# Attention, ELU projection and maxout layer on one core: order of stores, turns, splits and copies changed in the last three stages

## The chip, the cores and the metric

The kernel runs on one core of a Trainium2 chip. A core has TensorE (matmuls out of SBUF into PSUM), VectorE, ScalarE, GpSimd and SyncE, each with its own queue of instructions that it works off in order, and DMA engines that move data between HBM and SBUF. The metric is device time of one execution in microseconds (us). Before the change it is 539.83 us, the median of three runs (538.1 to 540.93).

## The reference

Three stages, all in float32 (the weight arrays of the second and third come as 64-bit floats):

```python
# 1. causal attention, batch 2, 12 heads, sequence 448, head size 64
scores = where(mask, -1e9, scale * q @ k.T)
attn = exp(scores - max(scores)); attn = attn / (sum(attn) + 1e-9)
x = (attn @ v) laid out as [896 tokens, 768]
# 2. ELU layer: 768 -> 2048 -> 768
h = x @ w_in                       # [896, 2048]
x = where(h > 0, h, exp(min(h, 0)) - 1) @ w_out
# 3. maxout layer: 768 -> 768 -> 768
h = maximum(maximum(x @ w1, x @ w2), x @ w3)
out = h @ w_out2                   # [896, 768]
```

## The kernel before, in words

**Products in three parts.** Each float32 operand is split into a high half (what TensorE's reduced format keeps, written by ScalarE) and a low half (the rest, a subtraction on VectorE); `split` (L129) does both. A product is then three matmuls: high x high, high x low, low x high.

**64-bit weights.** `load64` (L76) fetches a panel of 64-bit floats into a tile of the ring "raw" (three slots, L78). `conv64` (L87) turns it into float32 words: two ScalarE instructions (L91, L92) and two on VectorE in `join` (L96, L97). `conv_split` (L108) is `conv64` and `split` one behind the other. `weight_tile` is a ring of three ("ws"), `word_tile` a ring of two ("c").

**Stages.** Attention runs by a plan that is written out by hand. The ELU stage (L599 to L614) goes over 16 panels of w_in; 36 matmuls of a panel (`h_unit`, L350) give 128 columns of the hidden layer, which stay in SBUF. This stage is ordered by the framework's own scheduler. Everything behind L643 stands in a block of manual order: each engine gets its instructions in the order of the program.

**First output projection ("py", L667 to L693).** 24 panels of w_out (512 KB in HBM each): `load_wout(n + 3)`, `split_wout(n + 2)`, then 24 matmuls (L684) on panel n. Every four panels a block of 128 output columns is complete in PSUM; `y_copy` (ScalarE, L641) brings the block before to SBUF, and `y_first` or `y_sums` derive operands from it.

**Blocks turned in advance.** The 18 blocks of w1, w2 and w3 (768 KB each) are loaded beside the ELU and the py stage (`load_later`), turned into float32 (`turn_later`, two instructions on each of ScalarE and VectorE, into the one "ce" tile) and stored to a scratch area in HBM (L127). The store is issued by SyncE, in the same queue as the panel loads.

**Maxout stage.** The 896 tokens and the blocks are cut in 2 x 2 and multiplied with seven products in place of eight (x1 to x7, `product`, L746, nine matmuls each, L755). There are nine units n: `load_quad` (L708) fetches four quarter blocks of a unit from scratch, `split_first` splits two of them, `weight_sums` forms four sums and differences, `split_sums` and `split_last` split those. x1, x6, x7 and x4 add up in one PSUM bank, from which ScalarE copies the state after each (`keep_p`, `keep_u`, `keep_v`): the next product must not start before the copy. `result` and `result_x` add and take maxima on VectorE. `turn_half` (L854) loads, between the units, a half panel of w_out2 and turns it.

**Between py and the units** (L811 to L841) the operands that depend on the last y block are made; the last `y_copy` stands behind the splits there.

**Final stage.** `quadrant` and `rest` (L983) multiply by w_out2, again with seven products; `fill` splits an operand into a slot, the answers are added on VectorE and stored.

## Time and profile before

| | us |
|---|---|
| median of three runs | 539.83 |
| profiled execution | 542.84 |
| its span, first to last instruction | 541.0 |
| TensorE matmul busy | 491.7 (91%) |
| TensorE weight loads busy | 419.5 (78%) |
| VectorE busy | 386.8 (71%) |
| ScalarE busy | 316.7 (59%) |
| mean granted TensorE clock | 0.968 |

The profile is of one execution. In its rows PE is TensorE, PEld its weight loads, DVE VectorE, ACT ScalarE, POOL GpSimd, SP (SPq) the queue of SyncE; L350 is line 350 of the kernel. A row in order of time gives the start and the length in us, engine, line and operation, output<-input by the names in the program, and how many instructions it merges; in brackets stands the idle time of that engine before it and what ended it. A row of a window gives its start and end, its length, then busy time and count of PE, PEld, DVE, ACT and POOL, the granted TensorE clock (1.00 is 2.4 GHz), the DMA share and GB/s. Matmuls overlap, so the mean of one is longer than the distance from one to the next.

### The profile page before, as it was taken

What the parts mean: (1) busy time and instruction counts of PE and PEld (TensorE: products, weight loads), DVE (VectorE), ACT (ScalarE), POOL (GpSimd) and SP (SyncE); (2) the same over time, 40 slices, a digit from 0 to 9 for tenths busy, and PEclk for the clock granted to TensorE, in tenths of its full rate; (3) what the DMA queues carried; (4) which work ended last, traced back from release to release, by engine and by line L of the source; (5) the groups of instructions that cost most, each with busy time, mean ns of one, the idle gap of its engine ahead of it and who ended that gap; (6) DMA issues with size and microseconds to landing.
All of it is one profiled execution on the core that took longest, in us unless ns stands there. A gap on an engine that the chain in (4) does not pass through costs nothing.

```text
span 541.0 us, 7502 instructions
## 1 busy us (share of the span) xinstructions
PE 491.7 (91%) x2677; PEld 419.5 (78%) x2677; DVE 386.8 (71%) x759; ACT 316.7 (59%) x649; POOL 50.2 (9%) x104
## 2 busy tenths in 40 slices
PE   9999999999999999999988899029998999988997
PEld 5777677799999988898776677019987888878896
DVE  4999897698778786565555555286677777798874
ACT  4999897698888876354463553344434444334430
POOL 1656447000000000000000000000000000000000
PEclk9999999999999999999999999658999999998989
DMA  9996210158655450566665554522333332000104
GB/s 199 249 219 149 62 34 2 59 175 259 207 187 177 152 176 29 168 195 209 195 199 190 167 166 136 179 103 87 110 113 90 91 114 97 2 1 1 44 16 145
DMA packets 81509, 69.69 MB, mean 129 GB/s; under 512 B 35136, under 2 KB 75328, under 8 KB 81472
## 3 DMA queue, kind: packets, MB, share of 16 engines
q1 hardware_dynamic: 80544, 68.99, 43.3%
q8 instruction: 21, 0.34, 0.3%
q10 hardware_dynamic: 928, 0.23, 0.2%
q14 instruction: 16, 0.13, 0.1%
HBM read 59.38 MB, written 9.83 MB: 128 GB/s over the span
## 4 chain that ended last, share of the span: by engine, by line
PE 45%; DVE 21%; DMA 13%; ACT 13%; issue 4%; POOL 2%; SPq 1%; ACTq 0%; DVEq 0%; POOLq 0%
PE ph L350 21%; DMA raw_o<-in_moe_w_out_dram 7%; PE py L684 5%; PE s L227 4%; PE te L290 4%; DMA wx<-in_moe_w_out_dram 3%; DVE c_t L638 3%; PE av L315 3%; PE bx L755 3%; ACT wb L130 3%; POOL e L280 2%; DVE ce L96 2%; DVE ce L97 2%; ACT raw_e L92 2%; DMA out_dram<-o 1%
## 5 line engine op out<-in xcount | busy, mean ns | idle before, releaser
L684 PE MATMUL py<-gs,ws_o 128*128 128x512 f32 (+1 forms) x576 | 123.4, 369 | 8.0 <-ACT ws_o L130 6.4
L684 PEld LDWEIGHTS py<-gs,ws_o 128*128 128x128 f32 x576 | 102.8, 188 | 28.5 <-ACT ws_o L130 12.0
L350 PE MATMUL ph<-x,ws_l 128*128 128x512 f32 (+2 forms) x576 | 118.7, 365 | 0.0
L350 PEld LDWEIGHTS ph<-x,ws_l 128*128 128x128 f32 x576 | 103.9, 188 | 12.5 <-issue 1.0
L280 POOL TENSOR_SCALAR e<-e,r 112x336 f32<-112x336 f32 (+3 forms) x96 | 48.9, 528 | 42.6 <-DVE r L274 41.9
L261 ACT ACTIVATE e<-e,nm 112x448 f32<-112x448 f32 (+3 forms) x96 | 49.7, 526 | 3.3 <-DVE nm L247 3.1
L755 PE MATMUL bx<-ops_a_s,ws_a 128*128 128x448 f32 x81 | 20.7, 409 | 23.3 <-ACT y L641 23.3
L247 DVE CUSTOM_DVE_ANT_0 e<-s,mask 112x224 f32<-112x224 f32 (+3 forms) x96 | 37.8, 441 | 3.1 <-PE s L227 3.0
L755 PE MATMUL by<-ops_s,wb 128*128 128x448 f32 x162 | 36.9, 374 | 1.8 <-DVE r L638 1.8
L130 ACT ACTIVATE ws_o<-c_o 128x512 fp32r<-128x512 f32 x24 | 15.1, 630 | 39.8 <-DVE c_o L97 36.7
L755 PEld LDWEIGHTS bx<-ops_a_s,ws_a 128*128 128x128 f32 x81 | 17.5, 217 | 25.4 <-ACT y L641 23.7
L96 DVE SCALAR_TENSOR_TENSOR c_o<-c_o,raw_o 128x512 uint32<-128x512 uint32 x24 | 16.5, 688 | 25.4 <-ACT raw_o L92 25.4
L755 PEld LDWEIGHTS by<-ops_s,wb 128*128 128x128 f32 x162 | 30.9, 191 | 4.8 <-DVE r L638 2.2
L130 ACT ACTIVATE wb<-c_t 128x768 fp32r<-128x768 f32 x18 | 14.2, 836 | 26.9 <-DVE c_t L638 26.9
L96 DVE SCALAR_TENSOR_TENSOR ce<-ce,raw_e 128x768 uint32<-128x768 uint32 x18 | 17.2, 957 | 17.2 <-ACT raw_e L92 17.1
L131 DVE TENSOR_TENSOR ws_o<-c_o,ws_o 128x512 fp32r<-128x512 f32 x24 | 16.6, 692 | 18.0 <-ACT ws_o L130 18.0
L290 PE MATMUL te<-ident,e 112*112 112x112 f32 x240 | 27.7, 261 | 1.4 <-POOL e L280 1.2
L91 ACT ACTIVATE c_o<-raw_o 128x512 f32<-128x512 f32 x24 | 15.9, 664 | 20.2 <-DMA raw_o<-in_moe_w_out_dram 18.8
L290 PEld LDWEIGHTS te<-ident,e 112*112 112x112 f32 x240 | 23.8, 133 | 4.3 <-POOL e L280 2.8
L755 PE MATMUL bx<-ops_a,wb 128*128 128x448 f32 x81 | 18.8, 376 | 7.6 <-ACT v L641 7.6
L227 PE MATMUL s<-qk 64*112 64x224 f32 (+3 forms) x192 | 24.9, 405 | 0.0
L315 PE MATMUL av<-et,vn 112*64 112x448 f32 (+3 forms) x192 | 24.4, 403 | 0.0
(167 smaller groups left out, 862.1 us busy)
## 6 DMA issues: line engine op xcount, KB each, us to landing
raw_e<-in_moe_w_dram SPq DMA_DIRECT2D x18, 768.0 KB, 6.2
raw_l<-in_moe_w_in_dram SPq DMA_DIRECT2D x16, 768.0 KB, 4.7
raw_o<-in_moe_w_out_dram SPq DMA_DIRECT2D x24, 512.0 KB, 4.8
turned<-ce SPq DMA_DIRECT2D x18, 384.0 KB, 2.8
quad<-turned SPq DMA_DIRECT2D x18, 384.0 KB, 4.2
wx<-in_moe_w_out_dram SPq DMA_DIRECT2D x12, 384.0 KB, 3.1
qn<-in_q_dram SPq DMA_DIRECT2D x24, 112.0 KB, 3.8
vn<-in_v_dram SPq DMA_DIRECT2D x12, 224.0 KB, 3.9
```

The source lines that it names most:

```text
L96: nc.vector.scalar_tensor_tensor(r, r, 3, low, ALU.logical_shift_left, ALU.bitwise_or)
L130: nc.scalar.activation(hi, src, AF.Copy)
L131: nc.vector.tensor_tensor(lo, src, f32(hi), ALU.subtract)
L227: nc.tensor.matmul(s[j][:C, o : o + (c + 1) * C], qk[:, a, c * C : (c + 1) * C], qk[:, c2, : (c + 1) * C], start=(w == 0 and n == 0), stop ...
L247: nc.vector.tensor_tensor_reduce(out=e_t[h][:, EOFF[c] : EOFF[c] + (c + 1) * C], in0=ps_now.pop(("s", h, c)), in1=mask[:, (NCH - 1 - c) * ...
L261: nc.scalar.activation(e, e, AF.Exp, bias=nm_t[h][:, c : c + 1], scale=-1.0, accum_out=sm_t[p][:, j, c : c + 1],)
L280: nc.gpsimd.tensor_scalar(e, e, ps_now["r", h][:, c : c + 1], 1.0, ALU.mult, ALU.mult)
L290: nc.tensor.transpose(t[:C, n : n + C], e[:, EOFF[c] + j * C : EOFF[c] + (j + 1) * C], ident[:C, :C],)
L315: nc.tensor.matmul(a[j * D : (j + 1) * D, kc * C : S], vn[:, j * NCH + kc, :], et[j][:, TOFF[kc] : TOFF[kc] + S - kc * C], start=(n == 0), ...
L350: nc.tensor.matmul(ps, w(a, kc), x(c, kc), start=(i == 0), stop=(i == len(seq) - 1))
L684: nc.tensor.matmul(py[m, b][:, : at.stop - at.start], w[:, a, kc * P : (kc + 1) * P], g_sp[hk * HK + kc][:, c, at], start=(hk == 0 and i = ...
L755: nc.tensor.matmul(bank[:, :S], w, side[:, c, k, :], start=(not onto and k == 0 and (a, c) == (0, 0)), stop=(k == K2 - 1 and (a, c) == (1, ...
```

## The change

- Of the three "raw" slots two stay in the ring and one ("apart") is kept for the blocks turned in advance, for w_in panel 2, for every third quad and for the tile v of the final stage.
- Blocks are loaded at every odd panel of the ELU stage. In the py stage a block's store, and behind it the next block's load, are issued at the start of the panel after the turn; blocks are turned at odd panels.
- `conv_split` of a w_out panel is parted: in panel n the kernel splits panel n + 2, turns panel n + 3 and loads panel n + 5.
- The first three quads are loaded in the last panels of the py stage; between py and the units `split_first(0)`, `weight_sums(0)` and `split_first(1)` come first.
- In a unit, `turn_half`, `keep_v` and the c11 result go ahead of the sums' splits; the second `turn_half` goes ahead of x2.
- The last two units are written out and interleaved. The final stage's operand preparation is moved about, and the copy of l1 goes ahead of the t4 subtraction.

```diff
@@ -73,9 +73,12 @@
     NW = KD * P
     BIAS = 2.0**-112
 
-    def load64(key, src, n):
-
-        t = cv.tile([P, NW, 2], U32, tag="raw", bufs=3, name=f"raw_{key}")
+    def raw_tile(name, apart=False):
+        tag, bufs = ("apart", 1) if apart else ("raw", 2)
+        return cv.tile([P, NW, 2], U32, tag=tag, bufs=bufs, name=name)
+
+    def load64(key, src, n, apart=False):
+        t = raw_tile(f"raw_{key}", apart)
         k_n = src.shape[0] // P
         nc.sync.dma_start(
             t[:, :n, :].rearrange("p (k e) w -> p k (e w)", k=k_n),
@@ -112,17 +115,21 @@
     K2 = KF2 // 2
     scratch = ctx.enter_context(tc.tile_pool(name="scratch", bufs=1, space=DRAM))
     later = [(j + n * K2, i) for j in range(K2) for i in range(3) for n in range(2)]
-    loaded, turned = [], {}
+    loaded, leaving, turned = [], [], {}
 
     def load_later():
         m, i = later.pop(0)
-        raw = load64(f"e{m}_{i}", (w1, w2, w3)[i][:, m * P : (m + 1) * P], NW)
+        raw = load64(f"e{m}_{i}", (w1, w2, w3)[i][:, m * P : (m + 1) * P], NW, True)
         loaded.append((m, i, raw))
 
     def turn_later():
         m, i, raw = loaded.pop(0)
         c = cv.tile([P, NW], U32, tag="ce", bufs=1, name=f"ce{m}_{i}")
         conv64(raw, c, NW)
+        leaving.append((m, i, c))
+
+    def store_later():
+        m, i, c = leaving.pop(0)
         turned[m, i] = scratch.tile([P, NW], F32, name=f"turned{m}_{i}")
         nc.sync.dma_start(turned[m, i], f32(c[:, :]))
...
@@ -605,7 +612,8 @@
                 split_win(i, f"l{i}", f < 2)
         if loaded:
             turn_later()
-        if f > 3 and f % 2 == 0:
+            store_later()
+        if f % 2 == 1:
             load_later()
...
+    def turn_wout(i):
+        pan[i] = conv64(pan[i], word_tile(f"o{i}"), HK * P)
+
     def split_wout(i):
-        pan[i] = conv_split(f"o{i}", pan[i], HK * P)
-
-    for i in range(3):
-        load_wout(i)
-    for i in range(2):
-        split_wout(i)
+        c, pan[i] = pan[i], weight_tile(f"o{i}")
+        split(pan[i][:, 0, : HK * P], pan[i][:, 1, : HK * P], c)
+
+    load_wout(0)
+    load_wout(1)
+    turn_wout(0)
+    load_wout(2)
+    split_wout(0)
+    turn_wout(1)
+    load_wout(3)
+    split_wout(1)
+    turn_wout(2)
+    load_wout(4)
...
+        def load_quad(n):
+            j, i = ITEMS[n]
+            t = raw_tile(f"quad{n}", n % 3 == 2)
+            quads[n] = t = f32(t.rearrange("p n w -> p (n w)")).rearrange(
+                "p (q e) -> p q e", q=4
+            )
+            for x in range(2):
+                nc.sync.dma_start(
+                    t[:, 2 * x : 2 * x + 2].rearrange("p q e -> p (q e)"), turned[j + x * K2, i]
+                )
+
         for n in range(NP):
             m, hk = divmod(n, NQ)
-            if n + 3 < NP:
-                load_wout(n + 3)
+            if leaving:
+                store_later()
+                if later:
+                    load_later()
             if n + 2 < NP:
                 split_wout(n + 2)
-            if loaded:
+            if n + 3 < NP:
+                turn_wout(n + 3)
+            if n + 5 < NP:
+                load_wout(n + 5)
+            if n >= NP - 4 and n < NP - 1:
+                load_quad(n - NP + 4)
+            if n % 2 == 1 and loaded:
                 turn_later()
-            if hk % 2 == 0 and later:
-                load_later()
             if hk == 0:
...
+        split_first(0)
+        weight_sums(0)
+        split_first(1)
         part("a01", slice(0, 2), y[:, 3:5, T[0]])
         part("s2", slice(0, 2), y[:, 0:2, T[0]])
-        load_quad(0)
-        load_quad(1)
-        weight_sums(0)
-        split_first(0)
-        load_quad(2)
         part("s1", slice(0, 2), y[:, 0:2, T[1]])
         part("a11", slice(0, 2), y[:, 3:5, T[1]])
+        split_sums(0)
+        split_last(0)
         add(y[:, 3:5, T[0]], y[:, 3:5, T[0]], y[:, 0:2, T[0]], ALU.subtract)
         part("s4", slice(0, 2), y[:, 3:5, T[0]])
-        split_first(1)
-        split_sums(0)
-        split_last(0)
         y_copy(KD - 1)
...
-        for n in range(NI):
+        for n in range(NI - 2):
+            x6(n)
             if n > 0:
-                result(n - 1, 0, 1, U.pop(n - 1), Y.pop(n - 1))
+                result_c01(n - 1)
             if n + 3 < NI:
                 load_quad(n + 3)
-            if n + 2 < NI:
-                split_first(n + 2)
-            if n == NI - 2:
-                first_tiles()
-                for k in range(K2):
-                    first_part(k, 0)
-
-            Y[n] = bank3("by", n)
-            product("x5", n, Y[n], False)
+            split_first(n + 2)
+            x5(n)
             keep_u(n)
-            if n + 1 < NI:
-                weight_sums(n + 1)
-            if n == NI - 1:
-                tx = late.tile([P, 3, K2, DMO], F32, tag="wb", bufs=2, name="tx")
-                t1, t2, t3 = (tx[:, x] for x in range(3))
-                add(t1, Bq[0, 1], Bq[0, 0], ALU.subtract)
-                add(t3, Bq[1, 1], Bq[0, 1], ALU.subtract)
-                for k in range(K2 - 1):
-                    token_sums(k)
-
-            product("x7", n, X[n], True)
-            if n + 1 < NI:
-                split_sums(n + 1)
-            if n + 2 < NI:
-                x1(n + 2)
+            weight_sums(n + 1)
+            turn_half()
+            x7(n)
+            x1(n + 2)
             keep_v(n)
-            if n + 1 < NI:
-                split_last(n + 1)
-            else:
-                pair["x2"] = slot("a01"), slot("s2")
-                fill(pair["x2"][0], A[0, 1], slice(0, 2))
-                add(t2, Bq[1, 1], t1, ALU.subtract)
-            product("x4", n, X[n], True)
-            if n + 2 < NI:
-                keep_p(n + 2)
-            if n < NI - 1:
-                turn_half()
-            result(n, 1, 1, V.pop(n), Y[n])
-            if n + 2 < NI:
-                x2(n + 2)
+            result_c11(n)
+            split_sums(n + 1)
+            split_last(n + 1)
+            x4(n)
+            keep_p(n + 2)
+            turn_half()
+            x2(n + 2)
             result_x(n)
-            if n == NI - 2:
-                for k in range(K2):
-                    first_part(k, 1)
-            if n == NI - 1:
-                token_sums(K2 - 1)
-                split_left(0)
-                t = act.tile([P, 2, 2, K2, DMO], F32R, tag="x1", name="slot_x1")
-                pair["x7"] = t[:, 0], t[:, 1]
-                for k in range(K2):
-                    split(t[:, 0, 0, k], t[:, 0, 1, k], s3[k])
-            product("x3", n, Y[n], True)
-            if n + 2 < NI:
-                result(n + 2, 0, 0, p.pop(n + 2), Z.pop(n + 2))
-            if n < NI - 1:
-                turn_half()
+            x3(n)
+            result_c00(n + 2)
+
+        n = NI - 2
+        x6(n)
+        result_c01(n - 1)
+        x5(n)
+        keep_u(n)
+        weight_sums(n + 1)
+        split_sums(n + 1)
+        split_last(n + 1)
+        x7(n)
+        first_tiles()
+        x6(n + 1)
+        keep_v(n)
+        result_c11(n)
+        keep_u(n + 1)
+        x4(n)
+        for k in range(K2):
+            first_part(k, 0)
+        result_x(n)
+        x3(n)
+        for k in range(K2):
+            first_part(k, 1)
+        x7(n + 1)
+        result_c01(n)
+        keep_v(n + 1)
+        x5(n + 1)
+        tx = late.tile([P, 3, K2, DMO], F32, tag="wb", bufs=2, name="tx")
+        t1, t2, t3 = (tx[:, x] for x in range(3))
+        token_sums(0)
+        result_c11(n + 1)
+        x4(n + 1)
+        add(t1, Bq[0, 1], Bq[0, 0], ALU.subtract)
+        add(t3, Bq[1, 1], Bq[0, 1], ALU.subtract)
+        result_x(n + 1)
+        x3(n + 1)
+        split_left(0)
+        token_sums(1)
+        token_sums(2)
+        t = act.tile([P, 2, 2, K2, DMO], F32R, tag="x1", name="slot_x1")
+        pair["x7"] = t[:, 0], t[:, 1]
+        for k in range(K2):
+            split(t[:, 0, 0, k], t[:, 0, 1, k], s3[k])
...
@@ -1018,10 +1070,12 @@
         l1 = bank4("l1")
         rest(l1, f_b, 0, True)
         fill(pair["x7"][1], t3)
-        result(NI - 1, 0, 1, U.pop(NI - 1), Y.pop(NI - 1))
+        result_c01(NI - 1)
         for t in range(K2):
             copy(p1[:, t], x1[t])
-        fill(pair["x2"][0], A[0, 1], slice(2, 3))
+        add(t2, Bq[1, 1], t1, ALU.subtract)
+        pair["x2"] = slot("a01"), slot("s2")
+        fill(pair["x2"][0], A[0, 1])
         fill(pair["x2"][1], Bq[1, 0])
...
         fill(pair["x4"][0], A[1, 1])
-        t4 = Bq[1, 0]
-        add(t4, t4, t2, ALU.subtract)
-        fill(pair["x4"][1], t4)
         o = answer(0, 2, 0)
         copy(o, l1)
         store(o, LEFT.start, 0)
+        t4 = Bq[1, 0]
+        add(t4, t4, t2, ALU.subtract)
         for t in range(K2):
             add(u[:, t], p1[:, t], x6[t])
             add(v[:, t], u[:, t], x7[t])
+        fill(pair["x4"][1], t4)
```

## Rows read from the trace of the kernel before

**Rows 1.** Busy us (count) by stage and engine, granted clock, DMA share, GB/s
```profile
98.97:207.76 108.79, 108.79 (x542) 98.12 (x542) 86.83 (x121) 88.61 (x147) 0.00 (x0) 1.00 0.56 177
207.76:338.95 131.19, 123.22 (x577) 102.42 (x575) 73.45 (x101) 64.84 (x105) 0.00 (x0) 1.00 0.53 169
...
372.53:470.19 97.66, 91.46 (x443) 82.36 (x441) 72.13 (x121) 41.66 (x79) 0.00 (x0) 1.00 0.31 97
470.19:493.32 23.13, 19.93 (x91) 17.40 (x90) 21.64 (x35) 8.05 (x16) 0.00 (x0) 0.96 0.00 1
493.32:541.00 47.68, 41.72 (x226) 41.08 (x224) 31.69 (x45) 15.10 (x19) 0.00 (x0) 0.95 0.16 58
```

**Rows 2.** SyncE's DMA queue in order of time, py stage
```profile
265.02 0.34 SPq L127 DMA_DIRECT2D turned<-ce  x1
265.45 0.39 SPq L80 DMA_DIRECT2D raw_o<-in_moe_w_out_dram  x1
```

**Rows 3.** The page's DMA issues: size each, median us to landing
```profile
raw_e<-in_moe_w_dram SPq DMA_DIRECT2D x18, 768.0 KB, 6.2
raw_l<-in_moe_w_in_dram SPq DMA_DIRECT2D x16, 768.0 KB, 4.7
raw_o<-in_moe_w_out_dram SPq DMA_DIRECT2D x24, 512.0 KB, 4.8
...
quad<-turned SPq DMA_DIRECT2D x18, 384.0 KB, 4.2
wx<-in_moe_w_out_dram SPq DMA_DIRECT2D x12, 384.0 KB, 3.1
```

**Rows 4.** TensorE in order of time, from py to the units
```profile
333.47 5.52 PE L684 MATMUL py<-gs,ws_o 128*128 128x384 f32 x24 [0.88 <-ACT ws_o L130]
362.31 6.73 PE L755 MATMUL bx<-ops_a_s,ws_a 128*128 128x448 f32 x18 [23.32 <-ACT y L641]
```

**Rows 5.** ScalarE in order of time, the same stretch
```profile
342.57 0.89 ACT L91 ACTIVATE ce<-raw_e 128x768 f32<-128x768 f32 x1 [7.56 <-DMA raw_e<-in_moe_w_dram]
...
361.68 0.95 ACT L641 ACTIVATE y<-py 128x512 f32<-128x512 f32 x2
```

**Rows 6.** VectorE in order of time, the same stretch
```profile
354.23 0.95 DVE L131 TENSOR_TENSOR ws_a<-quad,ws_a 128x768 fp32r<-128x768 f32 x1
355.09 1.08 DVE L131 TENSOR_TENSOR ops_s<-y,ops_s 128x896 fp32r<-128x896 f32 x1
...
357.10 1.08 DVE L638 TENSOR_TENSOR y<-y 128x896 f32<-128x896 f32 x1
...
361.07 1.82 DVE L131 TENSOR_TENSOR wb<-c_t,wb 128x768 fp32r<-128x768 f32 x2
```

**Rows 7.** ScalarE in order of time, units
```profile
399.55 0.55 ACT L91 ACTIVATE wx<-wx 128x384 f32<-128x384 f32 x1 [4.40 <-DMA wx<-in_moe_w_out_dram]
...
405.80 1.58 ACT L130 ACTIVATE wb<-c_t 128x768 fp32r<-128x768 f32 x2 [4.11 <-DVE c_t L638]
```

**Rows 8.** TensorE in order of time, units
```profile
407.87 2.12 PE L755 MATMUL bx<-ops_a,wb 128*128 128x448 f32 x9 [1.36 <-ACT v L641]
```

**Rows 9.** Busy time of two units (columns as in rows 1)
```profile
372.53:385.29 12.76, 12.76 (x64) 11.83 (x63) 9.73 (x17) 5.02 (x10) 0.00 (x0) 1.00 0.39 124
...
399.05:413.45 14.40, 13.04 (x64) 11.68 (x63) 11.18 (x19) 5.87 (x11) 0.00 (x0) 1.00 0.35 111
```

**Rows 10.** TensorE in order of time, final stage
```profile
490.50 3.03 PE L755 MATMUL by<-ops_s,wb 128*128 128x448 f32 x9 [1.83 <-DVE r L638]
...
515.09 4.98 PE L983 MATMUL bxf<-slot_a,slot_s 128*128 128x384 f32 x18 [2.19 <-ACT o L641]
...
524.59 4.84 PE L983 MATMUL bzf<-slot_x 128*128 128x384 f32 x27
```

**Rows 11.** VectorE in order of time, last unit
```profile
481.85 2.62 DVE L638 TENSOR_TENSOR tx<-wx 128x1152 f32<-128x1152 f32 x2
...
484.97 1.15 DVE L638 TENSOR_TENSOR h<-h 128x384 f32<-128x384 f32 x2
```

More of the change, by code (lines that the diff above doesn't have):

```diff
@@ L337, in load_win @@
     def load_win(f, key):
-        raw_t[key] = load64(key, w_in[:, f * P : (f + 1) * P], NW)
+        raw_t[key] = load64(key, w_in[:, f * P : (f + 1) * P], NW, f == 2)
     def split_win(f, key, pin=False):
@@ L625, in load_wout @@
         )
+    def turn_wout(i):
+        pan[i] = conv64(pan[i], word_tile(f"o{i}"), HK * P)
     def split_wout(i):
-        pan[i] = conv_split(f"o{i}", pan[i], HK * P)
-    for i in range(3):
-        load_wout(i)
-    for i in range(2):
-        split_wout(i)
+        c, pan[i] = pan[i], weight_tile(f"o{i}")
[10 more added lines that the diff above has]
+    load_wout(4)
     T = HALVES
+    ITEMS = [(j, i) for j in range(K2) for i in range(3)]
+    NI = len(ITEMS)
     def add(out, x, y, op=ALU.add):
@@ L702, in tile_attention_elu_maxout @@
             ops[x] = late.tile([P, 2, K2, S], F32R, tag=x, name=f"ops_{x}")
-        ITEMS = [(j, i) for j in range(K2) for i in range(3)]
-        NI = len(ITEMS)
-        quads, sums, wa, wb = {}, {}, {}, {}
-        def load_quad(n):
-            j, i = ITEMS[n]
-            t = cv.tile([P, NW, 2], U32, tag="raw", bufs=3, name=f"quad{n}")
-            quads[n] = t = f32(t.rearrange("p n w -> p (n w)")).rearrange(
-                "p (q e) -> p q e", q=4
-            )
-            for x in range(2):
-                nc.sync.dma_start(
-                    t[:, 2 * x : 2 * x + 2].rearrange("p q e -> p (q e)"), turned[j + x * K2, i]
-                )
+        sums, wa, wb = {}, {}, {}
         def split_first(n):
@@ L906, in last_sums, with x6, x5, x7 @@
             add(A[0, 1][:, k], A[0, 1][:, k], A[0, 0][:, k], ALU.subtract)
-        for n in range(NI):
+        def x6(n):
             product("x6", n, X[n], True)
+        def x5(n):
+            Y[n] = bank3("by", n)
+            product("x5", n, Y[n], False)
+        def x7(n):
+            product("x7", n, X[n], True)
+        def x4(n):
+            product("x4", n, X[n], True)
+        def x3(n):
+            product("x3", n, Y[n], True)
+        def result_c00(n):
+            result(n, 0, 0, p.pop(n), Z.pop(n))
@@ L910, in tile_attention_elu_maxout, with result_c01, result_c11 @@
+        def result_c01(n):
+            result(n, 0, 1, U.pop(n), Y.pop(n))
+        def result_c11(n):
+            result(n, 1, 1, V.pop(n), Y[n])
+        for n in range(NI - 2):
+            x6(n)
             if n > 0:
-                result(n - 1, 0, 1, U.pop(n - 1), Y.pop(n - 1))
+                result_c01(n - 1)
             if n + 3 < NI:
                 load_quad(n + 3)
-            if n + 2 < NI:
-                split_first(n + 2)
-            if n == NI - 2:
-                first_tiles()
-                for k in range(K2):
-                    first_part(k, 0)
@@ L1007, in keep @@
         def keep(name):
-            t = cv.tile([P, NW, 2], U32, tag="raw", bufs=3, name=name)
+            t = raw_tile(name, name == "v")
             return f32(t.rearrange("p n w -> p (n w)"))[:, : K2 * DMO].rearrange(
```

1 line of the change is left out of this document (added).

## The prediction

> **What bounds the kernel now.** I read the busy times stage by stage first [rows 1]. In the ELU stage (98.97 to 207.76) TensorE runs without a gap: 540 matmuls (the window's count has two more at its edges) in 108.79 us, 0.2015 us each. I take this as the pace TensorE can hold when nothing is late. The stage behind it, the first output projection ("py"), has 576 matmuls of the same average width, so at that pace it needs 576 x 0.2015 = 116.0 us; it takes 131.19. So 15.2 us of it are waiting, though TensorE looks 94% busy there (a matmul whose weights are late is drawn long). Neither VectorE (73.45) nor ScalarE (64.84) nor DMA (share 0.53) fills that stage, so what is missing is order, not capacity.
>
> The Trainium skill ("Perfetto Trace Analysis", Identifying the Most-Contended Engine) says that matmul busy time is a bad measure of the distance to the roof and weight-load busy time a good one. The rows agree: weight loads are 98.12 of 108.79 us in the ELU stage and 102.42 of 131.19 here. By gaps between matmuls alone this stage would have 8.0 us to give and the sum below would be 7.2 us higher.
>
> The order of the SyncE queue shows why [rows 2]: the store of a turned block (L127) stands ahead of the next panel load (L80), and that load leaves 0.43 us behind the store, which itself has to wait until VectorE has joined the block. The load then takes 4.8 us [rows 3], the panel is turned and split only then, and TensorE waits.
>
> Then the largest hole: the last py matmul ends at 333.47 + 5.52 = 338.99 and the next matmul starts at 362.31 after 23.32 us [rows 4]. ScalarE waits 7.56 us for the last raw block [rows 5], and after it everything is done in a row: store, quad loads, splits, and as the last of them the copy of y out of PSUM at 361.68; x1(0) starts when its first half is done [rows 4, 5]. That wait ends on the copy because x1 gets the PSUM bank of the last py tile.
>
> In the nine maxout units ScalarE waits 4.40 us for the w_out2 half (turn_half), and 4.11 us for the weight sums; keep_v stands behind both, and x4 waits for keep_v, 1.36 us in the row shown [rows 7, 8]. The first unit, which has no such wait, takes 12.76 us for its 63 matmuls with TensorE always busy; a later one takes 14.40 [rows 9]. All seven up to x6(7) take 97.66 [rows 1].
>
> **The change, part by part.** Times are of the profiled execution: span 541.0 us, 542.84 with what lies around it.
>
> *ELU stage: 0.* Eight blocks are loaded in it instead of six, so one or two more are turned: 1.9 us of VectorE and 1.7 us of ScalarE each, beside 86.83 and 88.61 of 108.79 [rows 1]. The raw ring has two slots, the third is kept for the blocks. A slot turns every two panels, 14.5 us; a load lands in 4.7 us [rows 3] and conversion needs some 4 us. Without that cover each us of delay per panel would cost 13 us. Bounds: -1 to +5; I take 0.
>
> *py stage: -15.2.* Store and next block load are issued at the start of the panel after the turn, so no panel load stands behind a fresh store, and a panel is turned three and loaded five ahead. A panel is 24 x 0.2015 = 4.84 us. Within it, ScalarE splits panel n+2 (0.6), turns n+3 (1.2), VectorE follows and ends some 3.5 us into the panel; then load n+5 goes out, landing at 8.3, or 9.7 if it takes the 6.2 us of the 768 KB loads [rows 3]. Its turn starts at 4.84 x 2 + 0.6 = 10.3, and TensorE needs the result two panels later still. VectorE's 73.45 us and ScalarE's 64.84 [rows 1] fit beside 116 us. The wait added is that of a block's second turn for the store of the first (one "ce" slot); behind it on ScalarE stand the next split and the y copies, with a panel and more to spare. Bounds: 8.0 (only the gaps go) and 15.2 (all goes); I take 15.2, because slack is over 4.84 us at each step.
>
> *Transition: -17.4 of idle, -1.0 of clock.* Quads 0 to 2 are loaded at panels 20 to 22, landing 4.2 us later [rows 3]; the first two quads are in before the last panel. Call E the end of the last py matmul. wa(0) may be split when panel 21 is done, wa(1) when panel 22 is done, E-4.84; behind that wait, on both engines, stand all the parts. From there VectorE does in a row: wa(1) low half (starts E-3.9, 0.87), four parts of 896 columns (1.0 each), the sums' low halves (1.74), the last quarter (0.5, an estimate from its half width), the subtraction (1.08) [rows 6]: 8.2 us, to E+4.3. ScalarE then does s4's high half (0.9) and the first y copy (0.56 of the 0.95 [rows 5]), still the last of its row, so x1(0) starts at E+5.9 instead of E+23.3. Bounds: if the parts' memory came free only with the last panel, E+9.3; if VectorE's waits overlap better, E+4.5. The first 18 matmuls behind the long pause took 6.73 us, half rate, the lower clock level of 1.2 GHz [rows 4], 3.1 more than at full rate. Behind pauses of 1.83 and 2.19 us nine and eighteen matmuls lose 1.2 and 1.9 us at that level (the first of them 0.7 more in the group behind) [rows 10]; for 5.9 us I take 2.1 instead of 3.1.
>
> The Trainium skill ("TensorE: Matmul & The Clock Gate", What's actually happening) has it that the slow clock is the default and activity lifts it, which speaks against counting a shortened pause in full. The rows agree: a shorter pause still costs nearly the clock loss of a long one. Without such a loss behind short pauses the sum would be some 4 us lower.
>
> *Seven units: -7.7.* Keep_v now has one turn_half before it and no weight sums. With t from the start of x6(n) and 1.82 us for nine matmuls: keep_u 2.0 to 2.6; half turned on ScalarE 2.6 to 3.5; x7 ends 5.5, keep_v 5.7 to 6.2; x4 wants it at 7.3. So the wait goes. The half's DMA (3.1 us [rows 3]) leaves when the previous turn has been joined and lands about 1.5 us into the unit. Next bound is VectorE: up to 11.18 us of work per unit [rows 9], plus about 0.9 waiting for keep_v: 12.1 to 12.6 against 12.76. Tight; I take 12.85 x 7 = 90.0 instead of 97.66. Bounds: 89.3 and 97.7.
>
> *Last two units and the end: -5.7.* Ten products take 18.2 us at full rate; from x6(7) to the final stage they took 23.13 [rows 1]. Interleaved, each keep has another unit's product to hide behind: 4.9 saved, and 0.7 of half clock that reached into the first quadrant. In the final stage the 2.19 us wait for the copy of l1 [rows 10] goes, since that copy is issued before the t4 subtraction, with the 1.9 us of clock behind it: 4.1. But VectorE arrives late: after x5(8) (14.8 us from x6(7)) it has c11 (1.2), t1 and t3 (2.6), result_x (0.55), the left split (1.1), six token sums (3.5), three splits (1.45), the fill of t3 (1.3), by the widths of [rows 11], ending at 26.5. TensorE is through f1 (27 matmuls, 4.7 of the 4.84 in [rows 10]) and l1 (a third of it) at 24.5. A new wait of 2.0 us with 1.9 us of clock: +3.9. Net 4.9 + 0.7 + 4.1 - 3.9 = 5.8, taken as 5.7. Bounds: 2 and 9.
>
> **Sum.** 15.2 + 17.4 + 1.0 + 7.7 + 5.7 = 47.0. Profiled: 542.84 - 47.0 = 495.8. The median of the runs is 3.0 us under the profiled one (539.83), so I predict 493 us.
>
> **Rivals.** (a) The py stage stays paced by its loads: two raw slots instead of three, and up to three transfers at once. For: SyncE is one queue, and a blocked panel load holds up the store and the block load behind it. Against: 2.2 MB in 9.7 us is 230 GB/s, and the stage ran at share 0.53 for 169 [rows 1]. It needs landing times beyond 6.7 us at every panel. All of it: 493 + 15 = 508.
> (b) VectorE becomes the bound of the units: 12.6 of 12.76 leaves little, and each wait that the order adds shows. At the old 13.95 a unit: 493 + 8 = 501.
> (c) Slower than before: the two-slot ring starves the ELU stage. Each w_in load waits until the panel two before it has been turned, and VectorE and ScalarE are 80% busy there [rows 1]. Place: the 13 panels behind the third. It eats the gain of 47 us from 3.6 us of delay per panel on, a slot cycle of 21.7 us instead of 14.5, when load and conversion sum to some 9; at 4 us per panel 545 us. Against: nothing in the stage waits now.
> (d) The copies don't move: y's copy is still behind seven splits on ScalarE, and if the parts wait for the last panel's memory, idle is 9.3: 496.
>
> **How the numbers follow.** Forecast 0.70, (a) 0.09, (b) 0.10, (d) 0.06, (c) 0.03; 0.02 for no net change. The range takes the lower bounds' ends together in part (py and idle full, units 89.3, end 9: 487) and reaches up over (b) and (a): 486 to 508. Faster by over 0.5% (2.7 us, about what can be told from no change) 0.95, within it 0.02, slower 0.03.
>
> **What would show it.** py stage: 576 matmuls in about 116 us, with the panel load no longer next to the store. Between the last py matmul and x1(0): about 6 us, ended by ScalarE's y copy. Units at 12.8 us, with no x4 wait on v; if they are at 13.5 or more with VectorE back to back, (b). A new gap of about 2 us before the second quadrant group of the final stage. The ELU stage at 108.8 us; any TensorE wait there for ws_l speaks for (c). The forecast is wrong if the long hole shrinks by less than 10 us.

## The result

500.23 us, median of four runs (499.08 to 500.44), against 540.38 for the kernel before measured beside it (four runs, 538.1 to 541.91): a ratio of 0.926 (95% interval 0.922 to 0.929). The forecast was 493, its range 486 to 508. The profiled execution took 500.33, its span 498.5, 4.5 more than the sum had it (542.84 - 47.0 = 495.8, less the 1.8 around the span: 494.0).

The stages of the kernel after, columns as in [rows 1]: ELU, py, the first x's behind the seam, seven units, the last two, the final stage.

```profile
98.97:207.77 108.80, 108.80 (x542) 98.03 (x541) 87.83 (x121) 89.11 (x148) 0.00 (x0) 1.00 0.59 188
207.77:323.93 116.16, 116.16 (x577) 104.09 (x575) 81.13 (x113) 70.71 (x114) 0.00 (x0) 1.00 0.64 212
329.75:339.40 9.65, 9.65 (x37) 8.68 (x37) 5.46 (x10) 4.68 (x9) 0.00 (x0) 0.75 0.00 0
339.40:430.54 91.14, 91.14 (x443) 82.77 (x441) 72.08 (x120) 40.66 (x76) 0.00 (x0) 1.00 0.32 104
430.54:449.14 18.60, 18.60 (x92) 16.89 (x90) 15.72 (x26) 6.66 (x13) 0.00 (x0) 1.00 0.00 1
449.14:498.50 49.36, 40.33 (x226) 38.73 (x224) 37.45 (x53) 17.52 (x22) 0.00 (x0) 1.00 0.16 56
```

Set these beside [rows 1]: in py and in both unit stages TensorE's busy time now equals the length, so nothing waits there. What is left is the hole between 323.93 and 329.75, and 9 us of the final stage. TensorE has four waits over 1 us behind attention; here they are in order of time:

```profile
329.75 6.09 PE L781 MATMUL bx<-ops_a_s,ws_a 128*128 128x448 f32 x18 [5.82 <-ACT y L661]
...
457.22 1.68 PE L1035 MATMUL bxf<-slot_x 128*128 128x384 f32 x8 [1.50 <-DVE slot_x L138]
...
471.30 1.83 PE L1035 MATMUL bxf<-slot_a,slot_s 128*128 128x384 f32 x9 [1.09 <-ACT o L661]
474.45 1.85 PE L1035 MATMUL bxf<-slot_a,slot_s 128*128 128x384 f32 x9 [1.32 <-DVE v L658]
```

ScalarE, in order of time, at the hole and in the final stage:

```profile
328.27 0.95 ACT L137 ACTIVATE ops_s<-y 128x896 fp32r<-128x896 f32 x1 [3.00 <-DVE y L658]
329.12 0.96 ACT L661 ACTIVATE y<-py 128x512 f32<-128x512 f32 x2
...
470.75 0.49 ACT L661 ACTIVATE o<-bxl 128x384 f32<-128x384 f32 x1 [4.45 <-DMA out_dram<-o]
```

y's copy is still the last of ScalarE's row, at 329.12 instead of 361.68 [rows 5]. The copy of l1 (o<-bxl) no longer stands behind the t4 subtraction, but waits 4.45 us for the store of an earlier answer: it needs the slot (the tile that it writes), which is free when the store has landed.

### The profile page after: what moved, and what is told of

It reads as the page before. It is cut to its first block, busy times and chain, and to the rows that moved or that the text cites. A ratio compares the mean times of both kernels' runs of the same rounds, so it can differ in the third digit from the quotient of the medians.

```text
span 498.5 us, 7505 instructions
## 1 busy us (share of the span) xinstructions
PE 480.9 (96%) x2677; PEld 418.0 (84%) x2677; DVE 386.9 (78%) x758; ACT 316.1 (63%) x648; POOL 50.5 (10%) x104
## 4 chain that ended last, share of the span: by engine, by line
PE 84%; DVE 9%; ACT 3%; POOL 2%; DMA 1%; issue 1%; DVEq 0%; ACTq 0%; POOLq 0%
PE ph L357 23%; PE py L723 22%; PE bx L781 14%; PE by L781 6%; PE s L234 4%; PE te L297 4%; PE bz L781 3%; PE av L322 3%; POOL e L287 2%; ACT e L268 1%; DMA out_dram<-o 1%; DVE h L658 1%; DVE slot_x L138 1%; PE idle L448 1%; PE bzf L1035 1%; PE tk L196 1%
## 5 line engine op out<-in xcount | busy, mean ns | idle before, releaser
L723 PE MATMUL py<-gs,ws_o 128*128 128x512 f32 (+1 forms) x576 | 116.2, 363 | 0.0
L723 PEld LDWEIGHTS py<-gs,ws_o 128*128 128x128 f32 x576 | 104.3, 188 | 11.7
L287 POOL TENSOR_SCALAR e<-e,r 112x336 f32<-112x336 f32 (+3 forms) x96 | 49.1, 532 | 42.6 <-DVE r L281 41.9
L661 ACT ACTIVATE u<-bx 128x448 f32<-128x448 f32 x9 | 4.9, 546 | 36.0 <-PE bx L781 36.0
L138 DVE TENSOR_TENSOR gs<-g,gs 128x512 fp32r<-128x512 f32 (+2 forms) x30 | 18.7, 622 | 6.9 <-ACT gs L137 6.7
L137 ACT ACTIVATE gs<-g 128x512 fp32r<-128x512 f32 (+2 forms) x30 | 17.2, 574 | 8.7 <-DVE g L373 8.7
```

What stands on the lines that cost most here:

```text
L137: nc.scalar.activation(hi, src, AF.Copy)
L138: nc.vector.tensor_tensor(lo, src, f32(hi), ALU.subtract)
L287: nc.gpsimd.tensor_scalar(e, e, ps_now["r", h][:, c : c + 1], 1.0, ALU.mult, ALU.mult)
L723: nc.tensor.matmul(py[m, b][:, : at.stop - at.start], w[:, a, kc * P : (kc + 1) * P], g_sp[hk * HK + kc][:, c, at], start=(hk == 0 and i = ...
```

## The experiments

The theory at first: py is fast because panels are loaded, turned and split earlier (the lead); the seam follows from that and from the new order; the units from keep_v's place. The rivals: the late store does it; the early quads do it; VectorE or the clock sets the rest. Line numbers are each kernel's own.

**e1: the store at once, behind the turn; the lead kept.**

```diff
-            if leaving:
-                store_later()
-                if later:
-                    load_later()
+            if n % 2 == 0 and n > 0 and later:
+                load_later()
...
                 turn_later()
+                store_later()
```

> The changed kernel with one thing undone: in the py stage a block's store is issued right behind its turn again, in the same panel, instead of one panel late. Lead theory: the old loop was store -> panel load (4.8 us) -> turn and split of that panel -> turn of the next block -> its store, 12.4 us for two panels that TensorE works off in 9.7. What breaks it is that the load behind a store is now for a panel five ahead, so that nothing of the next block's turn waits for it. Then the late store does nothing: py stage 116 us, total 500 us. Rival, the queue theory: what helps is that a panel load no longer stands behind a fresh store; then the py stage goes back towards 131 us, total up to 515 us.

498.31 us, span 496.5; py 116.2 us, hole 5.82, both as in the kernel after. But the edit is no test of the store's place: between its two places SyncE has no other instruction, so the queue keeps the order of the kernel after, and the stores leave at the same times within 0.7 us. SyncE in the kernel after, then here:

```profile
276.32 0.34 SPq L134 DMA_DIRECT2D turned<-ce  x1
276.75 0.39 SPq L83 DMA_DIRECT2D raw_e<-in_moe_w_dram  x1
278.89 5.20 SPq L83 DMA_DIRECT2D raw_o<-in_moe_w_out_dram  x2
```

```profile
276.29 0.34 SPq L134 DMA_DIRECT2D turned<-ce  x1
```

What the change did to the queue is to put the block load between the store and the panel loads; they still stand behind the store, and the store still waits for the turn of its block (29.6 us in all in py, 112.6 in the kernel before). Nothing on TensorE waits for that now, and this is what speaks against the queue theory. The 1.9 us less are in the units: 1.824 us per nine matmuls instead of 1.86 (last section).

**e2: the lead undone, the late store kept.**

```diff
...
+            if n + 3 < NP:
+                load_wout(n + 3)
             if n + 2 < NP:
+                turn_wout(n + 2)
                 split_wout(n + 2)
-            if n + 3 < NP:
-                turn_wout(n + 3)
-            if n + 5 < NP:
-                load_wout(n + 5)
...
```

> The changed kernel with the other half of the py stage undone: panel n + 3 is loaded in panel n, and turning and splitting of panel n + 2 stand together again; stores stay one panel late. Lead theory: the loop is closed again (block's turn -> store -> load of panel n + 3 -> its turn and split in panel n + 1 -> next block's turn), 12 us for two panels: py stage 125 to 131 us, total 509 to 516 us. Queue theory: py stage stays at 116 to 118 us, total 500 to 502 us.

538.53 us, span 536.7: more than either theory gave. py takes 153.35 us, 22 more than in the kernel before. (It has two raw slots for its panels where the kernel before has three; that this makes the difference is argued, not tried.) TensorE, then SyncE's queue, then the chain of waits there:

```profile
255.92 11.39 PE L719 MATMUL py<-gs,ws_o 128*128 128x384 f32 x48 [3.47 <-ACT ws_o L137]
269.75 11.32 PE L719 MATMUL py<-gs,ws_o 128*128 128x384 f32 x48 [2.44 <-ACT ws_o L137]
```

```profile
287.46 0.34 SPq L134 DMA_DIRECT2D turned<-ce  x1
287.89 0.39 SPq L83 DMA_DIRECT2D raw_e<-in_moe_w_dram  x1
288.33 1.37 SPq L83 DMA_DIRECT2D raw_o<-in_moe_w_out_dram  x2
301.22 0.34 SPq L134 DMA_DIRECT2D turned<-ce  x1
```

```profile
288.33 5.88 DMA raw_o<-in_moe_w_out_dram
...
297.52 0.89 ACT ce L94
```

The loop is closed: store, block load, two panel loads together; 5.88 us for the load; the turn of one panel and the start of its split; the block's turn; and the next store can leave at 301.22, 13.8 us after the last, for two panels that TensorE does in 9.7. So without the lead all of py's gain is gone, and more, though the queue has the order of the kernel after (store, block load, panel loads).

The hole behind py is yet far from the 23.32 us of the kernel before:

```profile
369.85 6.30 PE L777 MATMUL bx<-ops_a_s,ws_a 128*128 128x448 f32 x18 [8.93 <-ACT y L658]
```

**e3: the old order between py and the units, quads loaded behind py's loop.**

```diff
-            if n >= NP - 4 and n < NP - 1:
-                load_quad(n - NP + 4)
...
-        split_first(0)
-        weight_sums(0)
-        split_first(1)
         part("a01", slice(0, 2), y[:, 3:5, T[0]])
         part("s2", slice(0, 2), y[:, 0:2, T[0]])
+        load_quad(0)
+        load_quad(1)
+        weight_sums(0)
+        split_first(0)
+        load_quad(2)
...
```

> The changed kernel with the order between py stage and units undone: the three quads are loaded behind the py loop, weight sums and first splits between the parts as before, y copy still last on ScalarE. Theory: the hole of 23.3 us was made by the last block, which was turned 5 us behind the end of the py stage; now it is turned 10 us before it, SyncE is free and issues the quad loads then, wherever they stand in the program. Then TensorE idles 5 to 7 us here, as in the changed kernel (5.8), total 499 to 502 us. Rival: the new order of the splits and the early quad loads made the gain; then TensorE idles 12 us or more, total 507 us or more. Beside it: nine matmuls of a unit took 1.83 us in the kernel before and 1.86 in the changed one; if they are at 1.83 here, the lead-in decides that pace.

501.04 us; TensorE at the seam:

```profile
330.73 5.83 PE L779 MATMUL bx<-ops_a_s,ws_a 128*128 128x448 f32 x18 [6.64 <-ACT y L661]
```

6.64 us of hole instead of 5.82. The order is worth 0.8 us of 17.5. SyncE has nothing else to do by then and issues all six quad loads from 314.64 on, 9.4 us ahead of py's end, though they stand behind py's loop in the program (in the kernel after four of them leave at 306.02).

What moved the hole is the store of the last block, behind which the quad loads stand in the queue. That store in the kernel before, then that store and y's copy here:

```profile
346.23 0.34 SPq L127 DMA_DIRECT2D turned<-ce  x1
```

```profile
314.25 0.34 SPq L134 DMA_DIRECT2D turned<-ce  x1
```

```profile
330.10 0.95 ACT L661 ACTIVATE y<-py 128x512 f32<-128x512 f32 x2
```

From the store to the copy, through the quads and all that is made of them, it is 15.5 us in the kernel before (copy at 361.68 [rows 5]) and 15.9 here. But the store leaves 7.3 us behind py's end there and 9.8 ahead of it here. Two things can have moved it: the engines are no longer behind, and the program turns the last block in panel 21 of py (counted from 0) instead of 23, since one block more is turned in the ELU stage and the turns stand at odd panels. In e2, without the lead, the store leaves at 357.40, 3.5 us ahead of py's end. No run puts the blocks alone back.

**e4: the old order in the first seven units.**

```diff
             weight_sums(n + 1)
-            turn_half()
             x7(n)
+            split_sums(n + 1)
             x1(n + 2)
             keep_v(n)
-            result_c11(n)
-            split_sums(n + 1)
             split_last(n + 1)
             x4(n)
...
```

> The changed kernel with the order inside the first seven units undone (weight sums' splits ahead of keep_v, both half panels late in the unit). Theory: x4 waits for keep_v again by 0.7 to 1.4 us in most units, the seven take 97 to 99 us instead of 91.1, total 506 to 508 us. Rival: with the quads early and VectorE not late any more the wait does not come back, 91 to 93 us, total 500 to 502 us. Pace of nine matmuls: 1.83 us says that the 1.86 of the changed kernel belongs to its unit order, 1.86 that it comes from outside the units.

506.26 us. Of TensorE's waits (total, times, longest) the kernel after has none like

```profile
PE bx L781 <- ACT v L661: 6.7, 6, 1.5
```

and the units take 97.87 us (338.88 to 436.75) instead of 91.14. So the wait for keep_v comes back, as the theory had it. That the six waits sum to the difference, 6.7 us, is chance: all but one of these units have the faster pace, at which seven take 89.4 us (e7), so the waits cost more than their length, some 8.3 us.

**e5: the old order of the last two units and the final stage.**

```diff
-        n = NI - 2
-        x6(n)
...
+        for n in (NI - 2, NI - 1):
+            x6(n)
+            result_c01(n - 1)
...
+            x5(n)
+            keep_u(n)
...
```

> The last two units one behind the other and the old order of the final stage's operands, everything else as in the changed kernel. From the start of x6(7) to the end the kernel before took 70.8 us and the changed one 68.0. Theory (the interleave is worth some 4.5 us, and the final stage gives 1.7 of it back, since the copy of l1 and the second quadrant group wait there): 2 to 3 us more than the changed kernel, about 503, with waits of 1.8 and 2.2 us back in the last unit and ahead of x4 in the final stage, each followed by matmuls at half rate. Rival (the interleave is worth the 5.7 us of the prediction, and the shortfall arose in the seven units alone): 506. TensorE's two paces may shift either by up to 1.9 us.

500.83 us, below both. From x6(7) on it takes 69.34 us, the kernel after 67.96. Its last two units and its final stage:

```profile
429.66:451.94 22.28, 19.14 (x91) 16.66 (x90) 20.82 (x34) 7.23 (x14) 0.00 (x0) 1.00 0.00 0
451.94:499.00 47.06, 41.04 (x226) 40.39 (x224) 32.49 (x46) 15.95 (x21) 0.00 (x0) 0.94 0.17 59
```

Interleaving saves 22.28 - 18.60 = 3.7 us, the new final stage costs 49.36 - 47.06 = 2.3. Of these 2.3, 1.0 lie ahead of the last nine matmuls (they start 42.6 us into the stage, here 41.6: three waits of 3.9 us in all against one of 2.24 with half rate behind it), 1.3 between them and the end.

**e6: y's copy and x1's operands first, the sums' splits behind.**

```diff
         part("a11", slice(0, 2), y[:, 3:5, T[1]])
-        split_sums(0)
-        split_last(0)
-        add(y[:, 3:5, T[0]], y[:, 3:5, T[0]], y[:, 0:2, T[0]], ALU.subtract)
-        part("s4", slice(0, 2), y[:, 3:5, T[0]])
         y_copy(KD - 1)
...
         part("s1", 2, y[:, 2, T[1]])
+        split_sums(0)
+        split_last(0)
...
```

> Between py and the units, the copy of the last y block is issued ahead of the sums' splits, and the operands of x1(0) and x1(1) first of all, those of x6(0) last. Theory (the 5.8 us hole is ScalarE's order alone: y's copy stands last in its row): x1(0) starts within 1 us of the last py matmul, no half rate behind it, and x6(0) starts 8 to 9 us after the last py matmul instead of 15.5; total about 493. Rival (VectorE's row of low halves is what x6(0) needs in any order): the hole moves to a place behind x1 or x2, x6(0) starts at 13 us or later, total 498 or more.

494.83 us, some 2 of the gain for the faster pace in the units. TensorE, then ScalarE behind the seam:

```profile
324.71 3.91 PE L781 MATMUL bx<-ops_a_s,ws_a 128*128 128x448 f32 x18 [0.69 <-ACT y L661]
...
332.12 1.99 PE L781 MATMUL bx<-ops_s,wb 128*128 128x448 f32 x9
...
337.95 3.58 PE L781 MATMUL bx<-ops_a_s,wb 128*128 128x448 f32 x9 [2.02 <-ACT u L661]
```

```profile
336.16 0.58 ACT L137 ACTIVATE ops_s<-y 128x448 fp32r<-128x448 f32 x1 [1.70 <-DVE y L658]
336.64 0.83 ACT L137 ACTIVATE ws_a<-quad 128x768 fp32r<-128x768 f32 x1
337.37 0.52 ACT L661 ACTIVATE u<-bx 128x448 f32<-128x448 f32 x1
```

The theory holds at its place: hole 0.69, full rate at once, x6(0) 8.1 us behind py's end instead of 15.5. Half of it is given back, since the copy of u now stands behind s4's split, which waits for VectorE: 2.02 us and nine matmuls at half rate.

**e7: answers take turns over both pairs of slots.**

```diff
+        turns = [0]
+
         def answer(t, tok, n):
-            return wk.tile([P, 512], F32, tag=f"mx{n}", ...
+            turns[0] ^= 1
+            return wk.tile([P, 512], F32, tag=f"mx{turns[0]}", ...
```

> The answers of the final stage take turns over both pairs of slots, so no answer waits for a store that has just been issued. Theory (the copy of l1 waits for a slot whose store must land, 4.45 us on ScalarE): ScalarE's wait for the store goes, and of the two pauses of 1.09 and 1.32 us ahead of x4 and x5 at least the first; 1.5 to 2.4 us less than the changed kernel at the same TensorE pace, about 498. Rival (VectorE's chain of additions is behind anyway, and the slot only covers it): the waits are renamed to VectorE and the time stays within 0.7 us.

494.42 us, 5.9 less than the kernel after, 2 of them for the faster pace. The final stage takes 46.2 us (446.38 to 492.6) instead of 49.36, a gain of 3.1 us where 1.5 to 2.4 were expected. ScalarE, then TensorE:

```profile
465.99 0.49 ACT L661 ACTIVATE o<-bxl 128x384 f32<-128x384 f32 x1 [2.37 <-PE bxl L1035]
```

```profile
467.36 1.72 PE L1035 MATMUL bxf<-slot_a,slot_s 128*128 128x384 f32 x9
470.13 1.84 PE L1035 MATMUL bxf<-slot_a,slot_s 128*128 128x384 f32 x9 [1.05 <-DVE v L658]
```

l1's copy now waits for its matmuls alone, and the pause of 1.09 us is gone; the one of 1.32, ended by VectorE, is 1.05. (Both lie within the quadrant of x6.) That is half of the gain; the other half is at the end (last matmul to last store 3.5 us, not 5.0: there too an answer waited for a slot).

**e8: t1 added just ahead of t2, not in the last unit.**

```diff
-        add(t1, Bq[0, 1], Bq[0, 0], ALU.subtract)
         add(t3, Bq[1, 1], Bq[0, 1], ALU.subtract)
...
-        add(t2, Bq[1, 1], t1, ALU.subtract)
...
         split_left(1)
+        add(t1, Bq[0, 1], Bq[0, 0], ALU.subtract)
+        add(t2, Bq[1, 1], t1, ALU.subtract)
```

> The addition for t1 (1.3 us of VectorE) is moved from the last unit to just ahead of t2 in the final stage, so that the operands of the second quadrant group are done earlier. Theory (that group waits 1.50 us because VectorE has a row of work ahead of its operands): the wait shrinks to 0.2 to 0.5 us and the kernel is 1.0 to 1.3 us faster at the same TensorE pace. Rival (VectorE is the bound of the whole final stage): the wait comes back whole further on, ahead of x2 or x4, and the time is the same within 0.4 us.

500.14 us at the faster pace, so slower by 2. TensorE:

```profile
453.98 1.66 PE L1034 MATMUL bxf<-slot_x 128*128 128x384 f32 x8 [0.31 <-DVE slot_x L138]
...
470.77 2.87 PE L1034 MATMUL bxf<-slot_a,slot_s 128*128 128x384 f32 x9 [3.82 <-ACT o L661]
```

1.50 became 0.31 as the theory says, and 1.09 became 3.82: TensorE came to that bank 1.2 us earlier (18.1 us into the stage, not 19.3), VectorE to the answers 1.5 later (20.1, not 18.5), and l1's copy still had to wait for their slot (until 470.23, ended by a store). The rival is right about the wait, which comes back more than whole; the same time within 0.4 us, which it had, is not what was measured.

**e10: the change up to py's end alone;** the edits of e3, e4 and e5 together.

```diff
-        split_first(0)
-        weight_sums(0)
-        split_first(1)
...
-            turn_half()
             x7(n)
+            split_sums(n + 1)
...
+        for n in (NI - 2, NI - 1):
+            x6(n)
...
```

> Of the change only the edits up to the end of py are kept: the raw slots, the late store, split and turn parted and the lead of three and five panels. The order between py and the units, the seven units, the last two and the final stage are the old ones. Theory (the lead is what counts, and it also empties most of the hole behind py, since the last block is turned and stored long before): py 116 us, hole 6 to 7 us, units and end as in the kernel before, so 539 - 15.1 - 16.7 - 0.6 = 507, within 2 us for TensorE's two paces. Rival (the hole needs the new order and the early quads as well, and the earlier runs hid it because one of the two was enough): a hole of 15 us or more, 516.

506.01 us: py 116.2, and the hole smaller than with the whole change:

```profile
328.06 5.65 PE L779 MATMUL bx<-ops_a_s,ws_a 128*128 128x448 f32 x18 [5.22 <-ACT y L661]
```

The program is that of e3 up to the units, and its hole is 1.4 us shorter: the quad loads left at 313.29 and VectorE had the first of them 4.7 us later, not 6.0. So the 0.8 us of e3 are within what the quads' landing varies. The edits to ELU and py bring 34 us of some 40, with the old seam (539.82 for the kernel before beside it).

**e11: e6, e7 and the parts of e8 that have room.** s4's operands go into the first unit, t1 takes the pause where t2 stood, two token sums move behind x2's operands, the first u and v go ahead of t4.

```diff
             keep_u(n)
+            if n == 0:
+                s4()
...
-        add(t2, Bq[1, 1], t1, ALU.subtract)
+        add(t1, Bq[0, 1], Bq[0, 0], ALU.subtract)
         pair["x2"] = slot("a01"), slot("s2")
...
+        for k in (1, 2):
+            more_sums(k)
         split_left(1)
+        add(t2, Bq[1, 1], t1, ALU.subtract)
```

> The changed kernel with four more edits: y's copy and the operands of x1 first in the seam, with the operands of x3(0) moved into the first unit so that the copy of u does not stand behind them; answers take turns over the slots; t1 goes into VectorE's pause ahead of x2's operands and two of three token sums behind them; the first u and v additions go ahead of t4. Theory (each wait is an order of one engine): x6(0) starts 8.1 us after py's end with no wait ahead of x7(0) (7.4 us less), the final stage has no wait above 0.4 us (3.1 + 1.6 + 1.0 us less), in all 500 - 13 = 487, and 485 at the faster TensorE pace. Rival (VectorE is the bound from py's end on, in the first unit and the final stage): the waits come back elsewhere, of 2 us or more in the first unit and again in the final stage, and the time is 491 or more.

489.37 us (488.61 to 490.08), between the two. Two longer waits are left. TensorE, then ScalarE:

```profile
341.14 2.53 PE L781 MATMUL bx<-ops_a,wb 128*128 128x448 f32 x9 [2.55 <-ACT v L661]
343.47 3.18 PE L781 MATMUL bz<-ops_a,ws_a 128*128 128x448 f32 x9
...
465.78 1.86 PE L1041 MATMUL bxf<-slot_a,slot_s 128*128 128x384 f32 x9 [2.17 <-DVE v L658]
```

```profile
339.68 0.54 ACT L94 ACTIVATE wx<-wx 128x384 f32<-128x384 f32 x1 [4.68 <-DMA wx<-in_moe_w_out_dram]
340.13 0.53 ACT L95 ACTIVATE wx<-wx 128x384 uint32<-128x384 uint8 x1
340.56 0.53 ACT L661 ACTIVATE v<-bx 128x448 f32<-128x448 f32 x1
```

wx has y's memory, so its first load waits for the last read of y, which s4 now does in the unit; v's copy is queued behind the turn of that load.

**e12: those two waits.**

```diff
-            turn_half()
+            if n > 0:
+                turn_half()
             x7(n)
             x1(n + 2)
             keep_v(n)
+            if n == 0:
+                turn_half()
...
+        add(u[:, 0], p1[:, 0], x6[0])
+        add(v[:, 0], u[:, 0], x7[0])
         for t in range(K2):
             o = answer(t, 0, 0)
```

> The version before it still has two waits: 2.55 us ahead of x4(0), because the copy of v stands behind the first turned half of w_out2, whose load waits until y has been read for the last time (both have the same memory); and 2.17 us ahead of the last third of x6's quadrant, for the first v addition. Here the first half is turned behind the copy of v, and the first u and v additions stand ahead of the three answers. Theory (each wait is the order of one engine): both waits go, with the 1.9 us at half rate behind the first; 4.7 to 6.6 us less than 489.4, so 483 to 485. Rival (VectorE or ScalarE has no room left, the late halves are late for the units behind): waits of 1 us or more appear ahead of x6(1) or x4(1), or ahead of x5 in the final stage, and the time is 487 or more.

486.07 us (485.88 to 487.35), a ratio to the kernel before of 0.899 (0.896 to 0.902), 14.2 us under the change. The first wait went whole (x4(0) follows at 338.96 without one); of the second, 2.17 us, 1.24 are left, one third of the quadrant earlier:

```profile
338.96 1.99 PE L781 MATMUL bx<-ops_a,wb 128*128 128x448 f32 x9
...
460.28 3.39 PE L1044 MATMUL bxf<-slot_a,slot_s 128*128 128x384 f32 x18 [1.24 <-DVE v L658]
```

That is 1 us above the expectation; TensorE's other waits from py on are 0.69 and 0.23 us.

**The changed kernel once more.**

> The changed kernel once more, for TensorE's pace in the units: 1.86 us per nine matmuls in the first profile. If the pace belongs to the program, each unit is 13.02 us again and the total within 0.5 us of 500.3. If it is drawn anew at a pause of each execution, units of 12.76 us and about 498.5 are to be seen as likely as not.

499.35 us; a unit is again 13.02 us (351.45 to 364.47). Two of two at 1.86 are too few to say that the pace belongs to the program, and e1, with the same order on each engine from py on, has 1.824.

## Why the prediction was right, and by how much not

| term | predicted | measured, from the windows |
|---|---|---|
| ELU stage | 0 | 0.0 |
| py | -15.2 | 131.19 - 116.16 = -15.0 |
| seam: idle and clock | -18.4 | 33.58 - 15.47 = -18.1 |
| seven units | -7.7 | 97.66 - 91.14 = -6.5 |
| last two units | -4.9 | 23.13 - 18.60 = -4.5 |
| final stage | -0.9 | 47.68 to 49.36 = +1.7 |
| sum (541.0 to 498.5) | -47.0 | -42.5 |

The two last terms are parted by the windows: the 0.7 us of half clock lie in the final stage. Together they were 5.8, taken as 5.7.

**py: number right, cause half right.** The prediction read the store ahead of the panel load [rows 2] as the reason for the waiting, and had it that "no panel load stands behind a fresh store" any more. It still does, with a block load between (278.89 behind 276.32), and nothing waits; e2 has that same queue without the lead and loses everything. What counts is the lead, how many panels ahead a panel is loaded and turned; e2 takes back both at once and has one raw slot fewer than the kernel before, so their shares are open, and no run changes the store's place in the queue alone. That the stage would give 15 us, and not the 8.0 of its gaps, came from matmul counts and the ELU stage's pace: 123.22 us of busy time became 116.16 with the same matmuls. The Trainium skill ("Perfetto Trace Analysis", Identifying the Most-Contended Engine) warns of matmul busy time as a measure of the distance to the roof; these two numbers agree.

**Seam: right to 0.3 us, and ScalarE's y copy ends it, as said.** But the early quads and the new order that the prediction costed are worth 0.8 us (e3), or less than nothing (e10, 5.22 us). What emptied the hole is that the last block is stored 9.4 us ahead of py's end and not 7.3 behind it, so the 7.56 us wait for its raw tile [rows 5] and the row behind it lie beside py's matmuls; how much of this the lead does and how much the earlier turn is open. Rival (d), 9.3 us of idle, did not come. The clock came out at 6.73 - 6.09 = 0.6 of the expected 1.0.

**Units: mechanism right, size off by 1.2.** The term "12.85 x 7" took 1.82 us for nine matmuls from the rows of before; TensorE did them in 1.86, so 13.02 x 7. The same pace makes 0.4 us in the last two units (18.60 instead of 18.2). At 1.824 (e7: 338.76 to 428.14) the seven take 89.4, the lower bound. VectorE, rival (b), does not show.

**The end: the step that failed.** "In the final stage the 2.19 us wait for the copy of l1 [rows 10] goes, since that copy is issued before the t4 subtraction, with the 1.9 us of clock behind it: 4.1." The copy's own operand was free; its destination was not: three answers and l1's share two slots, and the store has to land first, so 1.09 us of the wait stayed. Behind it VectorE's v addition was late as well, 1.32 us, which the prediction had not looked for. The new wait ahead of the second quadrant came, 1.50 us of the 2.0, without the 1.9 of clock. Up to the last nine matmuls the stage is 1.3 us above the forecast (they start 42.6 us into it; before, 42.2, less the 0.9 forecast). Another 1.3 lie between them and the end, for which the prediction had no term (6.8 us, before 5.5). With other slots for the answers (e7) 1.6 us go in each of the two parts.

**From the profile to the median.** The 3.0 us between the profiled run of before and its median were taken off the forecast; after, that distance is 0.1 (500.33 and 500.23). That and the 4.5 us above make the 7.2 that the forecast was low, to 0.2 us of rounding (the forecast was 492.8, given as 493).

## What to carry to other kernels

These three come from one kernel; they say where to look first. Where a stage of steady matmuls takes longer than their count at the pace of an undisturbed stage, count how many steps ahead the load, the conversion and the split of an operand are issued, and lengthen that lead before touching the order of the queue. A copy that is moved ahead on its engine is only early if its destination is free too: look up whose slots it takes and which store must land first, including tiles that have another's memory. When one wait is taken away, follow the same engine's queue to the next thing that stands behind its new place; e6, e8 and e11 each gave back a part or all in this way.

## What the runs showed of the hardware

**Two paces of TensorE.** The stream of 128x448 matmuls runs at 1.86 or at 1.824 us per nine, at a granted clock of 1.00 in both, and keeps one for hundreds of matmuls. TensorE in the unit stage of e5, where it changes at a wait of 0.69 us:

```profile
431.52 2.02 PE L781 MATMUL by<-ops_s,wb 128*128 128x448 f32 x9
433.38 2.02 PE L781 MATMUL bx<-ops_a_s,wb 128*128 128x448 f32 x9
436.09 2.09 PE L781 MATMUL bx<-ops_a,wb 128*128 128x448 f32 x9 [0.69 <-ACT v L661]
438.02 1.99 PE L781 MATMUL by<-ops_s,wb 128*128 128x448 f32 x9
439.85 1.99 PE L781 MATMUL bx<-ops_s,wb 128*128 128x448 f32 x9
```

The distance of the starts is 1.86 ahead of the wait and 1.83 behind it. The kernel after (twice), e3, and e5 and e10 up to their first wait in the units show 1.86; e1, e2, e6, e7, e8, e11 and e12 1.824; e4 changes for one unit. It is worth 2 us of the units, as much as some of the edits here. e1 has the same instructions in the same order on each engine from py on as the kernel after, and e7 up to the final stage, and both have the other pace; so that order does not choose it. Units without any transfer (the last two of the kernel after) run at 1.86 as well. What chooses it stays open.

**The length of a wait alone does not tell whether the clock falls.** The 2.02 us of e6 and the 2.55 of e11 were followed by matmuls at half rate, the 1.2 GHz level; the 2.17 of e11 was not (nine matmuls in 1.70 us), nor the 1.50 of the kernel after, whose final stage has 1.00 granted throughout. The Trainium skill ("TensorE: Matmul & The Clock Gate", What's actually happening) has the slow clock as the default that activity lifts. The stretch behind the 5.82 us hole, at 0.75, agrees; the 1.9 us that the prediction charged to the final stage's new wait did not come.
